# RG-LRU and soft mixture of experts on one core: one exponential for the decays of two units, and a new plan

## The chip, the cores and the metric

The kernel runs on one core of a Trainium2 chip. The metric is the device time of one execution in microseconds (us). Engines: PE (TensorE), DVE (VectorE), ACT (ScalarE), POOL (GpSimd) and SP (SyncE, which only issues transfers here). Each engine runs its own instructions strictly in the order in which they were written; semaphores hold an instruction until what it reads is there.

## The reference, cut to what matters

```python
# B, S, D = 4, 5056, 256; 8 experts, 4 slots each, hidden width 1024; all float32
log_a = 8 * sigmoid(r_gate) * log(clip(sigmoid(a_param)))      # negative
a_t   = exp(log_a)                                             # the decay
norm  = sqrt(max(1 - a_t * a_t, 1e-6))
xg    = norm * sigmoid(i_gate) * x
for t in range(S):                                             # a scan along the sequence
    h = a_t[:, t] * h + xg[:, t];  y[:, t] = h
x = y.reshape(B * S, D)                                        # 20224 tokens
logits = x @ phi                                               # 32 slots
d = softmax(logits, over tokens);  slot_input = d.T @ x
slot_out[e] = relu(slot_input[e] @ w1[e]) @ w2[e]              # per expert
out = softmax(logits, over slots) @ slot_out
```

## The kernel before, in words

**Tiling.** The 20224 tokens are 40 *quads* of 512 tokens (the last has 256). A *unit* is two quads, but the first and the last unit have one; there are 21 units, and a *chunk* is two units (`CHUNKS`), the last one. The three inputs come in quads of 512 KB, tokens on partitions. PE transposes them so that the 256 channels lie on partitions in two halves `h` and time runs along the row.

**One unit, step by step** (task names of the plan and lines of the profile):

- `TR` (L559, PE): transposes r into a double PSUM buffer `pair`; `SR` (L570, ACT): tanh of it into the decay tile `A`, a buffer of the class `b`. A sigmoid is had from tanh here.
- `EX` (L612, ACT): the exponential with a scale and a bias per channel, in place, one instruction per half, so two per unit over 1024 elements each.
- `SQ` (L623, POOL): squares the decay into `N`. `RT` (L639, ACT): the root, over both halves at once (2048 elements).
- `SI` (ACT): the gate i, in one of three ways by the letter of `IV` for the unit. S is a sigmoid (L583); P is tanh (L585) and a correction `P1` on POOL (L592); E is tanh, whose correction is put into the sum: PE transposes and adds two tiles. `U` (L601, POOL): gate times x.
- `TU` (L658, PE): transposes that product into `pair`. `ST` (L675, DVE): times the root. `SC` (L692, DVE): the scan, one per half.
- `TY` (L716, PE) turns y back to tokens on partitions, two blocks of 128 tokens at a time, and `YC` copies it out of PSUM, on DVE (L732) or ACT (L730), whichever the plan gives it.
- For each group of four quads: `LG` (L772, PE) the logits, `LE` (L785, DVE) a running maximum, `LD`, `TE`, `ES` (L826, ACT) their exponentials, `AC` (L846, PE) the weighted sum, `AE` (L862, DVE) its accumulation.

**After the scans** the partial sums of four column groups are merged (`MT` to `SL`, L1023 to L1050), PE runs the experts' two layers (L1087, L1135), and the token-side softmax is multiplied with the slots' outputs (`CT` to `OT`, L1204 to L1292), copied out of PSUM (`OE`, L1304 on ACT, L1306 on DVE) and stored (`OD`, L1316).

**Tables.** ACT needs another function table for exp and tanh, for sigmoid, for sqrt; tanh is in the first two. A change of table is an instruction of its own, shown under the line that needs it.

**What sets the order.** `Planner` is a list scheduler that runs when the program is built. Each task has an engine, a duration and a latency that the author wrote down, its dependencies, a priority and the buffers it takes. The planner walks through time with those durations and hands out buffers; the order in which tasks begin in that plan is the order in which they are written into each engine's queue. ACT's main tasks don't follow priorities: their sequence `act_seq` is built from `phases`, for each chunk tanh and exponentials, then the sigmoids, then the roots. Loads follow the same sequence on SP's queue, with i and x of a quad side by side. Tasks of ACT outside the sequence (copies, `ES`) are put between by rules in `pick_act`.

**Buffers.** `st` (7 of 512 KB) hold r and i, `b` (16 of 1 MB) hold x, `A` and `N`, `yn` (8) hold y; in PSUM there are 3 `pair` and 2 single banks. A unit's decays and roots lie in whichever `b` buffer is free.

## Time and profile before

| | |
|---|---|
| time, median of 3 runs | 311.07 us (311.02 to 311.43) |
| the profiled execution | 311.99 us, of which 310.2 are its span |
| busy PE, DVE, ACT, POOL | 263.0, 253.2, 251.8, 216.6 us |
| moved by DMA | 78.94 MB read, 20.71 MB written |
| mean granted TensorE clock | 0.968 |

The span is what lies between the first and the last instruction. A row of a timeline gives the start in us from the span's start, the length, the engine, the line, the operation, what it writes and reads, how often, and in brackets how long the engine had stood idle before it and what ended that. A row of a group gives, behind the bar, busy us in all and the mean ns of one, then the idle time before the group. A row of waits gives us in all, how many, and the longest. A row of stages gives start and end, length, then busy us of each engine with its count of instructions, the granted TensorE clock, the DMA engines' share and GB/s.

### The profile page before, as it was taken

The page shows a single profiled execution, that of the slowest core. Times are in us where ns is not written, and L with a number is a line of the kernel's source. Part 1 is how long each engine was busy: PE and PEld are TensorE (multiplying, and loading weights), DVE is VectorE, ACT ScalarE, POOL GpSimd, SP SyncE. Part 2 cuts the span into 40 slices and gives each one's busy share as a digit, 9 for nine tenths or more (in the row PEclk, how much of TensorE's full clock was granted, in tenths as well). Part 3 has the DMA queues.
Part 4 walks back from the last instruction along what each step waited for, and adds up shares of the span by engine and source line. Part 5 has one row for each costly group of instructions (what it writes and reads, how often), then busy time and mean ns, then how long its engine had stood idle before and what let it go on. Part 6 is the DMA issues. An engine that isn't in the chain of part 4 may idle for free.

```text
span 310.2 us, 5828 instructions
## 1 busy us (share of the span) xinstructions
PE 263.0 (85%) x2181; PEld 199.5 (64%) x2181; DVE 253.2 (82%) x319; ACT 251.8 (81%) x282; POOL 216.6 (70%) x162
## 2 busy tenths in 40 slices
PE   4979959689698995977969979879998999999890
PEld 3979857675564854856647547564555578878770
DVE  0236579899999999888999999999987359999870
ACT  6699999999999999899899999999330038899560
POOL 4598979968979999999597999994304503347200
PEclk9999999799999999897999999979999999999995
DMA  6999649899997786768979978879999309999997
GB/s 228 416 408 403 244 164 409 335 363 359 391 411 282 295 296 238 277 250 298 410 268 300 368 257 309 272 262 398 404 386 386 130 0 379 401 406 406 394 408 284
DMA packets 30288, 100.03 MB, mean 322 GB/s; under 512 B 3378, under 2 KB 3380, under 8 KB 30260
## 3 DMA queue, kind: packets, MB, share of 16 engines
q1 hardware_dynamic: 30256, 99.66, 85.0%
q8 instruction: 17, 0.28, 0.3%
q14 instruction: 11, 0.09, 0.1%
q10 hardware_dynamic: 4, 0.00, 0.0%
HBM read 78.94 MB, written 20.71 MB: 321 GB/s over the span
## 4 chain that ended last, share of the span: by engine, by line
PE 35%; DVE 27%; ACT 18%; DMA 9%; issue 6%; POOL 2%; SPq 0%; DVEq 0%; ACTq 0%; POOLq 0%
DVE b L692 9%; DVE pair L675 7%; PE pair L658 6%; PE pair L559 5%; DMA out_dram<-st 5%; PE bank L1292 5%; DMA st<-in_r_gate_dram 4%; ACT b L639 3%; ACT b L612 3%; ACT b L570 3%; DVE yn L732 3%; PE one L716 3%; PE one L772 2%; PE one L1135 2%; ACT st L583 2%
## 5 line engine op out<-in xcount | busy, mean ns | idle before, releaser
L601 POOL TENSOR_TENSOR b<-st,b 128x1024 f32<-128x1024 f32 (+1 forms) x36 | 84.3, 2359 | 0.5
L692 DVE TENSOR_TENSOR_SCAN b<-b,b,pair 128x1024 f32<-128x1024 f32 (+4 forms) x40 | 82.4, 2063 | 0.5
L623 POOL TENSOR_TENSOR b<-b 128x1024 f32<-128x1024 f32 (+1 forms) x40 | 72.7, 1835 | 13.6 <-ACT b L612 12.0
L675 DVE SCALAR_TENSOR_TENSOR pair<-b,pair 128x1024 f32<-128x1024 f32 (+2 forms) x42 | 48.4, 1156 | 16.8 <-PE pair L658 7.8
L559 PE MATMUL pair<-ident,st 128*128 128x128 f32 x316 | 45.6, 290 | 14.4 <-DVE b L692 6.4
L559 PEld LDWEIGHTS pair<-ident,st 128*128 128x128 f32 x316 | 37.1, 148 | 22.6 <-DVE b L692 10.3
L612 ACT ACTIVATE b<-b,ca 128x1024 f32<-128x1024 f32 (+2 forms) x42 | 48.8, 1190 | 0.4
L658 PE MATMUL pair<-ident,b 128*128 128x128 f32 x316 | 45.5, 287 | 1.9 <-DVE b L692 1.7
L570 ACT ACTIVATE b<-pair 128x1024 f32<-128x1024 f32 (+1 forms) x40 | 40.1, 1010 | 5.8 <-PE pair L559 5.7
L716 PE MATMUL one<-ident,b 128*128 128x128 f32 x232 | 37.0, 295 | 8.1 <-DVE yn L732 4.7
L658 PEld LDWEIGHTS pair<-ident,b 128*128 128x128 f32 x316 | 37.8, 148 | 8.8 <-issue 5.1
L732 DVE COPY yn<-one 128x512 f32<-128x512 f32 x53 | 34.9, 684 | 4.0 <-PE one L716 3.9
L716 PEld LDWEIGHTS one<-ident,b 128*128 128x128 f32 x232 | 27.9, 149 | 15.5 <-DVE yn L732 7.8
L1292 PE MATMUL bank<-bd,hT 128*128 128x512 f32 x120 | 33.2, 401 | 1.0 <-DVE hT L1282 0.9
L639 ACT ACTIVATE b<-b 128x2048 f32<-128x2048 f32 (+2 forms) x19 | 33.3, 1794 | 0.3 <-POOL b L623 0.2
L1235 POOL TENSOR_TENSOR b<-b,rs_all 128x512 f32<-128x512 f32 (+2 forms) x11 | 10.6, 961 | 26.1 <-DVE rs_all L1227 21.6
L1292 PEld LDWEIGHTS bank<-bd,hT 128*128 128x128 f32 x120 | 21.7, 188 | 5.6 <-DVE hT L1282 1.2
L772 PE MATMUL one<-b,phi_sb 128*32 128x512 f32 (+1 forms) x164 | 24.3, 587 | 0.3 <-DVE yn L732 0.3
L846 PE MATMUL one<-yn,eS 128*32 128x257 f32 x304 | 22.8, 384 | 0.2 <-ACT eS L826 0.2
L1304 ACT COPY st<-bank 128x512 f32<-128x512 f32 x33 | 18.7, 594 | 4.3 <-PE bank L1292 3.7
L592 POOL TENSOR_SCALAR st<-st,half_sb 128x1024 f32<-128x1024 f32 (+1 forms) x14 | 15.2, 1092 | 9.9 <-ACT st L585 9.9
L1280 ACT CAST hT<-bank 128x512 fp32r<-128x512 f32 (+1 forms) x10 | 5.8, 579 | 19.7 <-PE bank L1269 19.6
(138 smaller groups left out, 436.0 us busy)
## 6 DMA issues: line engine op xcount, KB each, us to landing
st<-in_i_gate_dram SPq DMA_DIRECT2D x39, 512.0 KB, 5.3
b<-in_x_dram SPq DMA_DIRECT2D x39, 512.0 KB, 6.3
st<-in_r_gate_dram SPq DMA_DIRECT2D x38, 512.0 KB, 6.2
out_dram<-st SPq DMA_DIRECT2D x37, 512.0 KB, 5.3
b<-in_moe_w_dram SPq DMA_DIRECT2D x26, 512.0 KB, 9.3
st<-in_moe_w_dram SPq DMA_DIRECT2D x6, 512.0 KB, 4.5
st<-in_r_gate_dram SPq DMA_DIRECT2D x3, 256.0 KB, 2.9
out_dram<-st SPq DMA_DIRECT2D x3, 256.0 KB, 4.6
```

What stands on the lines that cost most here:

```text
L559: nc.tensor.transpose(out=o[:, m, :], in_=raw("r", q)[:, m * D + h * P : m * D + (h + 1) * P], identity=ident,)
L570: nc.scalar.activation(dst, t(rp)[:, :, :c], AF.Tanh, scale=0.5)
L601: eng.tensor_tensor(out=o, in0=a, in1=b, op=ALU.mult)
L612: nc.scalar.activation(v, v, AF.Exp, scale=ca[:, h : h + 1], bias=ca[:, h : h + 1])
L623: eng.tensor_tensor(out=t(Nb[p])[:, h, :c], in0=v, in1=v, op=ALU.mult)
L639: nc.scalar.activation(v, v, AF.Sqrt, bias=quarter if f != 1.0 else f, scale=-f)
L658: nc.tensor.matmul(o[:, m, :], raw(nm, q)[:, m * D + h * P : m * D + (h + 1) * P], ident, is_transpose=True, start=(nm == nms[0] and m == ...
L675: nc.vector.scalar_tensor_tensor(v, t(Nb[p])[:, h, :c], 0.5e-3 if gate_of(quads(p)[0]) == "E" else 1e-3, v, op0=ALU.max, op1=ALU.mult)
L692: nc.vector.tensor_tensor_scan(dst, dst, flat()[:, s0:s1], init, op0=ALU.mult, op1=ALU.add)
L716: nc.tensor.transpose(out=flat()[:, b * D + h * P : b * D + (h + 1) * P], in_=t(A[p])[:, h, o : o + P], identity=ident,)
L732: nc.vector.tensor_copy(out=dst, in_=v)
L1292: nc.tensor.matmul(t(op), t(hT)[:, b * P // 2 : (b + 2) * P // 2], T["bd"][part].rearrange("p i d -> p (i d)"), start=(part == 0), stop=(p ...
```

## The change

Five things are changed together.

1. **Decays side by side.** The 16 `b` buffers become 8 tiles of two. In each chunk with two full units the second unit's decay buffer is the *mate* of the first's: both are taken at once, in the two halves of one tile (`twin`, `take`). `EX` then is one instruction per half for both units, over 2x1024 elements, after the tanh of all four quads. Other buffers are handed out so that whole tiles stay free.
2. **The gates** (`IV`) are chosen anew: 13 units by sigmoid, 3 and not 2 by E, the others by P. 11 units were S before.
3. **The order in a chunk.** `PRE = 2`, `PRE0 = 3`: tanh of r for the first two quads of the next chunk (three after the first chunk) stand among the gates of this one, ahead of its roots. `SIM = 0`: the tanh gates are no longer mixed among the exponentials but follow them. `XLATE`: the loads of x of the first chunk come behind its gates' loads.
4. **Durations and priorities of the plan** change (`PEX`, the costs of `EX`, `LN` and the first loads; `TRP`, `YLAG`, `LGP`, `ACP`, `TUP`; `FILL`, which lets ACT take copies while it would wait), one `yn` buffer goes, more `b` buffers are kept back from x and `A`, and two tables shift single tasks in priority or in ACT's sequence.
5. **The first output** is stored in two halves (`ODS = 1`).

```diff
-PRE = 0
-PRE0 = 0
-IV = 'PPEESSSSSPPPSSSSPPSSP'
-YLAG = 6
+PRE = 2
+PRE0 = 3
+IV = 'PESESSSSSPPESPSSSSSSP'
+YLAG = 14
-FILL = False
-TRP = 20
+FILL = True
+TRP = 10
-TUP = 14
-ACP = 0
-LGP = 10
+TUP = 15
+ACP = -4
+LGP = 0
-N_YN = 8
-FING = 3
+N_YN = 7
+FING = 5
-XRES = 2
-ARES = 0
-SIM = 1
+XRES = 3
+ARES = 1
+SIM = 0
-PHI = 4
-XLATE = False
+PHI = 8
+XLATE = True
-EARLY = {}
-SHIFT = {}
+EARLY = {'TY37.2': 3.6, 'HP2.0': 10.0, 'SC13.0': 1.1, ...}
+SHIFT = {'SI5': 2.1, 'SR3': 1.1, 'SI27': 1.0, 'EX0.1': 4.1, ...}
+PEX = 1.03
+ODS = 1
...
+    def twin(self):
+        free = self.slots["b"]
+        return next((i for i in free if i % 2 == 0 and i + 1 in free), None)
...
+        elif b.mate is not None:
+            i = self.twin()
+            b.slot, b.mate.kept = [i], i + 1
...
-        make("b", N_B, [P, 2, 2 * QT], sb)
+        make("b", -(-N_B // 2), [P, 4, 2 * QT], sb)
+        T["b2"] = T["b"]
+        T["b"] = [b[:, i : i + 2, :] for b in T["b2"] for i in (0, 2)]
...
+    def mk_exh(p, h):
+        c = plen(p)
+        us = [p, p + 1] if p + 1 in second else [p]
+
+        def e_ex(h=h):
+            v = T["b2"][A[p].slot[0] // 2][:, h::2, :] if len(us) == 2 else t(A[p])[:, h, :c]
+            nc.scalar.activation(
+                v, v, AF.Exp, scale=ca[:, h : h + 1], bias=ca[:, h : h + 1]
+            )
+
+        EX[(p, h)] = add("ACT", f"EX{p}.{h}", 0.29 + 0.853 * c / 1024 * len(us),
+                         deps=[SR[q] for u in us for q in quads(u)] + [t_ca], ...)
...
+            cut = nb // 2 if (i * J + j) < ODS else nb
+            for k, b0 in enumerate(range(0, nb, cut)):
...
```

Three places in the built order. First ACT's queue at the start, from the second quad to the first change of table for a root. `pair` buffers hold transposed r, `st` the gate i, `b` the decays. Before:

```order
L570 ACTIVATE b_71<-pair_102 128x2x512
L585 ACTIVATE st_63<-st_63 128x1024
L612 ACTIVATE b_69<-b_69,ca 128x512
L570 ACTIVATE b_71<-pair_103 128x2x512
L585 ACTIVATE st_65<-st_65 128x1024
L612 ACTIVATE b_71<-b_71,ca 128x1024 x2
L585 ACTIVATE st_66<-st_66 128x1024
L639 ACT_TABLE_LOAD
```

And after:

```order
L621 ACTIVATE b_68<-pair_94 128x2x512
L621 ACTIVATE b_68<-pair_93 128x2x512
L685 ACTIVATE b_68<-b_68,ca 128x1024 x2
L636 ACTIVATE st_64<-st_64 128x1024
L685 ACTIVATE b_68<-b_68,ca 128x512
L636 ACTIVATE st_66<-st_66 128x1024
L621 ACTIVATE b_71<-pair_93 128x2x512
L621 ACTIVATE b_71<-pair_94 128x2x512
L636 ACTIVATE st_61<-st_61 128x1024
L621 ACTIVATE b_71<-pair_92 128x2x512
L702 ACT_TABLE_LOAD
```

The gates moved behind the exponentials of unit 1, and three tanh of the next chunk (`b_71`) moved ahead of the roots. On SP's queue the loads there are r0, r1, i0, x0, r2, i1, x1 before, and r0, r1, r2, i0, r3, i1, r4, i2, r5, x0, x1, x2 now.

Second, ACT's queue over the chunk of units 6 and 7, from the change to the table of exp and tanh to the change for the roots. Before:

```order
L570 ACT_TABLE_LOAD
L570 ACTIVATE b_74<-pair_102 128x2x512
L570 ACTIVATE b_74<-pair_103 128x2x512
L612 ACTIVATE b_74<-b_74,ca 128x1024
L570 ACTIVATE b_76<-pair_102 128x2x512
L612 ACTIVATE b_74<-b_74,ca 128x1024
L570 ACTIVATE b_76<-pair_101 128x2x512
L826 ACTIVATE eS_94<-one_96 128x512
L612 ACTIVATE b_76<-b_76,ca 128x1024 x2
L583 ACT_TABLE_LOAD
L583 ACTIVATE st_64<-st_64 128x1024
L583 ACTIVATE st_67<-st_67 128x1024
```

(two more gates follow, and then the roots). After:

```order
L621 ACT_TABLE_LOAD
L621 ACTIVATE b_74<-pair_94 128x2x512
L621 ACTIVATE b_74<-pair_92 128x2x512
L889 ACTIVATE eS_85<-one_88 128x512
L685 ACTIVATE b_74<-b_74,ca 128x2x1024 x2
L634 ACT_TABLE_LOAD
L634 ACTIVATE st_64<-st_64 128x1024
L634 ACTIVATE st_65<-st_65 128x1024
L621 ACTIVATE b_68<-pair_92 128x2x512
L634 ACTIVATE st_67<-st_67 128x1024
L634 ACTIVATE st_61<-st_61 128x1024
L621 ACTIVATE b_68<-pair_92 128x2x512
```

Two of four tanh left the front of the chunk, four exponentials became two, and two tanh of the next chunk (`b_68`) stand among the gates.

Third, PE's queue at the end of the scans: the transposes of the last quad's y (from its decay tile, `b_74` before and `b_69` now) against the weighted sums `AC` (32x257) of the last two groups. Before:

```order
L772 MATMUL one_97<-b_74,phi_sb 32x256
L846 MATMUL one_96<-yn_88,eS_95 32x257
L846 MATMUL one_96<-yn_89,eS_95 32x257
L846 MATMUL one_96<-yn_88,eS_95 32x257
L846 MATMUL one_96<-yn_89,eS_95 32x257
L1023 MATMUL bank_2177<-ident,M 1x128
L816 MATMUL bank_2178<-ident,lD_92 128x96 x2
L846 MATMUL one_96<-yn_88,eS_95 32x257
L846 MATMUL one_96<-yn_89,eS_95 32x257
L716 MATMUL bank_2179<-ident,b_74 128x128 x4
L1028 MATMUL bank_2177<-ones,mrep 128x1
L846 MATMUL bank_2180<-yn_90,eS_94 32x257 x2
```

After:

```order
L835 MATMUL one_87<-b_69,phi_sb 32x256
L779 MATMUL one_88<-ident,b_69 128x128 x4
L909 MATMUL bank_2138<-yn_77,eS_86 32x257
L909 MATMUL bank_2138<-yn_78,eS_86 32x257
L1094 MATMUL bank_2139<-ident,M 1x128
L879 MATMUL bank_2140<-ident,lD_83 128x96 x2
```

The transposes (`x4`) moved from behind the last but one group's sums to ahead of them.

More of the change, by code (lines that the diff above doesn't have):

```diff
@@ L535 @@
         xb[p].late = lambda pl, tag: len(pl.slots["b"]) > XRES
+        ib[p].late = lambda pl, tag: len(pl.slots["b"]) > XRES
+    second = set()
+    if EX2:
+        for ch in chunks:
+            full = [p for p in ch if plen(p) == 2 * QT]
+            second |= set(full[1::2])
+    for p in second:
+        A[p - 1].mate = A[p]
     yn = {q: Buf("yn", f"yn{q}") for q in range(NQ)}
@@ L585, in e_si @@
                 nc.scalar.activation(v, v, AF.Tanh, scale=0.5)
-        g = SI[q] = add("ACT", f"SI{q}", 0.07 + 0.22 * n, deps=[ld[("i", q)]], prio=q, emit=e_si,
-                        uses=[st[("i", q)]], kind="sig" if how == "S" else "tanh")
+        if two_i(p) and i:
+            g = SI[q] = SI[q - 1]
+        else:
+            qs = quads(p) if two_i(p) else [q]
+            g = SI[q] = add("ACT", f"SI{q}", 0.07 + 0.22 * n * len(qs), deps=[ld[("i", a)] for a in qs], prio=q, emit=e_si,
+                            uses=[st[("i", q)]], kind="sig" if how == "S" else "tanh")
         def e_p1():
@@ L907, with late_i, exs @@
     ahead = []
+    def late_i(q):
+        return two_i(unit[q][0]) and unit[q][1]
+    def exs(p):
+        return [] if p + 1 in second else [("EX", p - (p in second), h) for h in range(H)]
     def roots(k):
@@ L915 @@
             now = [("SR", q) for q in quads(p) if q not in ahead]
-            prev = [("EX", chunks[k][i - 1], h) for h in range(H)] if i else []
+            prev = exs(chunks[k][i - 1]) if i else []
             x += merge(prev, now)
-        x += [("EX", chunks[k][-1], h) for h in range(H)]
+        x += exs(chunks[k][-1])
         if SIM:
-            x = merge(x, [("SI", q) for q in cq[k] if gate_of(q) != "S"])
+            x = merge(x, [("SI", q) for q in cq[k] if gate_of(q) != "S" and not late_i(q)])
         phases.append(x)
@@ L941 @@
             elif it[0] == "SI":
-                order += [("i", it[1]), ("x", it[1])]
+                for q in quads(unit[it[1]][0]) if two_i(unit[it[1]][0]) else [it[1]]:
+                    order += [("i", q), ("x", q)]
         if XLATE and len(order) and k == (0 if GATES0 else 2):
```

80 lines of the change are left out of this document (53 added, 27 removed).

## Prediction

> **What bounds the kernel now.** I read the shares of the engines first, then one table of stages, then the waits, then single rows.
>
> ```profile
> PE 263.0 (85%) x2181; PEld 199.5 (64%) x2181; DVE 253.2 (82%) x319; ACT 251.8 (81%) x282; POOL 216.6 (70%) x162
> ```
>
> No engine is full over the span, so the stages are read apart. The columns are length, busy time of each engine with its count, granted TensorE clock, DMA share and GB/s.
>
> ```profile
> core 0: us, PE busy (x) PEld busy (x) DVE busy (x) ACT busy (x) POOL busy (x), PEclk, DMA share, GB/s
> 9.23:39.23 30.00, 27.11 (x239) 26.39 (x238) 13.66 (x12) 28.67 (x27) 26.90 (x15) 1.00 0.94 363
> 39.23:207.49 168.26, 139.31 (x1174) 103.71 (x1175) 159.68 (x163) 164.71 (x151) 152.80 (x83) 0.96 0.84 309
> 207.49:227.70 20.21, 19.84 (x176) 11.96 (x174) 20.06 (x23) 13.79 (x24) 8.58 (x9) 0.98 1.03 400
> 227.70:235.13 7.43, 6.32 (x51) 3.29 (x50) 4.52 (x14) 0.97 (x4) 1.05 (x2) 1.00 1.05 386
> 235.13:255.58 20.45, 20.29 (x294) 13.06 (x295) 11.79 (x26) 2.48 (x6) 7.21 (x6) 1.00 0.41 149
> 255.58:310.20 54.62, 45.29 (x237) 36.99 (x235) 42.47 (x81) 36.35 (x68) 16.43 (x16) 0.94 0.96 380
> ```
>
> The reader is to see four bounds in turn. From 39.23 to 207.49 us ACT is busy 164.71 of 168.26 and DVE 159.68: two engines share the bound, and each has little to give, 3.55 us idle on ACT and 8.58 on DVE. From 207.49 to 227.70 DVE alone is full (20.06 of 20.21): the multiply and the scans of units 18, 19 and 20. To 255.58 a chain of short PE and DVE steps runs. From there on the output transfers fill the DMA engines. So time comes out of the long stage only if both ACT and DVE are let go.
>
> ```profile
> DVE pair L675 <- PE pair L658: 7.8, 5, 2.0
> ACT b L570 <- PE pair L559: 5.7, 6, 1.6
> ```
>
> DVE's largest waits are for the transposed input of the multiply (7.8 us in five waits), ACT's for the transposed r gate (5.7 us in six). Those are what a new order can remove.
>
> **The change part by part.** *The exponentials.* 36 instructions over 1024 elements become 18 over 2x1024.
>
> ```profile
> L612 ACT ACTIVATE b<-b,ca 128x1024 f32<-128x1024 f32 x38 | 46.1, 1242 | 0.3
> L639 ACT ACTIVATE b<-b 128x2048 f32<-128x2048 f32 x17 | 31.7, 1906 | 0.3 <-POOL b L623 0.2
> L639 ACT ACTIVATE b<-b 128x1024 f32<-128x1024 f32 x1 | 1.1, 1062 | 0.0
> ...
> 32.56 2.38 ACT L612 ACTIVATE b<-b,ca 128x1024 f32<-128x1024 f32 x2
> ```
>
> Two in a row take 2.38 us where one takes 1.242, so a further one costs 1.14. No double one is in the trace; the nearest rows are the roots, which grow by 1.906 - 1.062 = 0.844 us for 1024 more elements. A double exponential in a row is then 1.14 + 0.84 = 1.98 against 2.28 for two: 0.30 saved. Bounds: 2.28, nothing saved; and 1.242 - 0.844 = 0.40 where nothing overlaps an instruction's fixed part. I take 0.30, as they stand in a row: 18 x 0.30 = 5.4 us off ACT.
>
> *Table loads.* Up to the root of unit 18 ACT has 29 loads in place of 27, because two more chunks take gates by sigmoid.
>
> ```profile
> 69.68 2.36 ACT L612 ACTIVATE b<-b,ca 128x1024 f32<-128x1024 f32 x2
> 72.06 1.28 ACT L583 ACT_TABLE_LOAD   x1
> 73.35 3.90 ACT L583 ACTIVATE st<-st 128x1024 f32<-128x1024 f32 x4
> ...
> 203.61 3.71 ACT L639 ACTIVATE b<-b 128x2048 f32<-128x2048 f32 x2
> ```
>
> The load at 72.06 is 1.28 us and the gate after it starts 0.01 us later, so 2 x 1.29 = 2.6 us come back. The Trainium skill, "ScalarE: Activation LUTs", section "What ACT_TABLE_LOAD costs", adds a drain of about 1.38 us to the 1.28 at every switch to another set; by that page the two would cost about 5.3 us, an estimate. Here the exponentials ended at 69.68 + 2.36 = 72.04, the load began 0.02 us later and the gate 0.01 us after it: the trace has no such gap, and the sum keeps 2.6.
>
> *The rest of ACT up to that root:* the last unit's tanh moved ahead of it (0.5) and one more copy (0.5). Net on ACT: -5.4 + 2.6 + 0.5 + 0.5 = -1.8 us. The root of unit 18 ends at 203.61 + 1.86 = 205.5 now.
>
> *The order within a chunk.* Two of the next chunk's four tanh now run before the roots, so exponentials follow the load after two tanh, not four. That lets POOL's squares begin earlier, and half of the transposes of r have a whole phase to be ready in: it is against ACT's 5.7 us. Take the window 9.23 to 207.49: ACT idles 1.33 + 3.55 = 4.9 us there. All, half or none may go; half is 2.4. Root 18 then ends at 205.5 - 1.8 - 2.4 = 201.3.
>
> *The start.* r0, r1, r2 are loaded first, each x of the first chunk after nine gate loads, and three tanh of the next chunk stand ahead of the first roots.
>
> ```profile
> 7.22 1.97 PE L559 MATMUL pair<-ident,st 128*128 128x128 f32 x8 [1.12 <-DMA st<-in_r_gate_dram]
> 13.14 1.02 ACT L570 ACTIVATE b<-pair 128x1024 f32<-128x1024 f32 x1 [1.24 <-PE pair L559]
> 37.19 3.90 ACT L639 ACTIVATE b<-b,quarter 128x2048 f32<-128x2048 f32 x2
> ...
> 20.73 1.29 DVE L675 SCALAR_TENSOR_TENSOR pair<-b,pair 128x512 f32<-128x512 f32 x2 [7.69 <-ACT b L639]
> 38.40 0.69 DVE L732 COPY yn<-one 128x512 f32<-128x512 f32 x1 [3.14 <-PE one L716]
> 39.23 1.23 DVE L675 SCALAR_TENSOR_TENSOR pair<-b,pair 128x1024 f32<-128x1024 f32 x1
> ...
> 35.13 3.77 POOL L623 TENSOR_TENSOR b<-b 128x1024 f32<-128x1024 f32 x2
> 56.63 7.04 POOL L601 TENSOR_TENSOR b<-st,b 128x1024 f32<-128x1024 f32 x3
> ```
>
> The wait of 1.24 at 13.14 is for r2, which came sixth and now comes third; it goes. At 363 GB/s 0.52 MB take 1.44 us, so x0, eight transfers behind r1 (there at 7.22), lands near 7.2 + 8 x 1.44 = 18.7 and is multiplied and transposed before the first root is out; were it later, each us would push DVE's first multiply by one. Until the first root ACT does three tanh more, 2.8 us (1.02 each, less some overlap), so DVE's first multiply moves from 20.73 to about 22.3. Up to the end of root 2 (39.1 now) ACT has two tanh and a load more and two exponentials merged twice: +1.9 + 1.3 - 0.5 - 1.24, so 40.5. Unit 2 now takes sigmoid, and its products stand on POOL behind four squares: the first square at about 28.3, four of them at 1.88 each (3.77 for two) to 35.8, the gates done then, two products at 2.35 (7.04 for three) to 40.6, a transpose of about 1 us: unit 2's multiply starts at about 42, not 39.23. That costs DVE 2.8 us, partly filled by the copies for which it waited 3.14 us at 38.40.
>
> *DVE from unit 2 to unit 18.* Counted in the order, 56 copies out of PSUM stand there and not 63; all else is equal in number.
>
> ```profile
> 24.98 1.29 DVE L732 COPY yn<-one 128x512 f32<-128x512 f32 x2 [0.73 <-PE one L716]
> ```
>
> A copy in a row costs 1.29 - 0.69 = 0.60, so DVE has 159.68 - 4.2 = 155.5 us of work. From 42 this gives unit 18's multiply at 197.5 with no idle, 206.1 with all 8.58, 201.8 with half. ACT says 201.3 and from there a wait for the transpose of up to the 2.0 that it is now (205.5 to 207.49); half of it gives 202.3, which I take: **5.2 us** off, between 1.4 (206.1) and 8.5 (ACT without idle, 205.5 - 1.8 - 4.9 = 198.8, and 0.2 to the multiply). Both rest on POOL, which has six gate corrections of 1.1 us fewer and one product of 2.35, 9.0 us in all; DVE makes that product in the 7.69 us before its first multiply. If squares or products are late on POOL, the multiply is what is late next (first rival). PE gets 16 transposes more for a third unit that sums the tanh gate there, 16 x 0.11 = 1.8 us of the 29 that it idles in the long stage.
>
> *The last scans.* One copy fewer stands between the multiply of 18 and the last scan: **0.6 us**.
>
> *The merge.* The last transposes of y are issued ahead of the last two groups' sums and not behind the first of them.
>
> ```profile
> 230.45 0.33 ACT L826 ACTIVATE eS<-bank 128x192 f32<-128x192 f32 x1 [0.79 <-PE bank L816]
> 231.54 0.69 DVE L732 COPY yn<-bank 128x512 f32<-128x512 f32 x1
> 231.74 1.60 PE L846 MATMUL bank<-yn,eS 128*32 128x257 f32 x12
> ```
>
> The last sum waits for the copy that ends at 232.2 though its weights were there at 230.8; about 1.2 us, of which I take **1.0**, between 0 and 1.2. Expert weights stand behind it:
>
> ```profile
> 242.00:244.00 2.00, 2.00 (x44) 1.23 (x40) 0.48 (x1) 0.00 (x0) 2.00 (x3) 1.00 0.48 176
> ...
> 246.20 4.52 PE L1135 MATMUL one<-b,b 128*32 128x256 f32 x80
> ```
>
> The transfers end near 243, and the last of five experts in these 4.52 us starts near 249.8, so 6.8 us of gain ahead of it are covered even if the weights come no earlier; past that they would set the end.
>
> *The outputs.* The first output leaves in two halves.
>
> ```profile
> 254.48 0.59 ACT L1304 COPY st<-one 128x512 f32<-128x512 f32 x1 [0.92 <-PE one L1292]
> 254.96 0.59 ACT L1304 COPY st<-bank 128x512 f32<-128x512 f32 x1
> ```
>
> It is issued at 255.58, where the last stage of the table begins, since it waits now for both copies (255.55); the first half is ready at 255.07, so the stream starts **0.5 us** earlier, between 0 and 0.6; the one extra issue is covered by transfers in flight. The moved copies there change which engine does them; with 380 GB/s over the stage I cost them at nothing.
>
> Sum: 5.2 + 0.6 + 1.0 + 0.5 = 7.3. The profiled execution took 311.99 (span 310.2), so it would take 304.7; the median of the runs, 311.07, is 0.92 below, so **303.8**.
>
> **The rivals.** *POOL late in every chunk (slower).* Both first squares now wait for the first double exponential and all products stand behind four squares. DVE waits five times now for transposed products, 2.0 us at most. With 2.0 at each of nine chunks that is 18 us of idle on DVE: 42 + 155.5 + 18 = 215.5, 8.0 later, less the other 2.1: 317.0. It decides from 12 us, 1.35 a chunk. For it: eight chunks take sigmoid, not six. Against: POOL idles 15.5 us in the long stage and has those 9.0 us less to do.
>
> *The stalls stay.* If the waits merely move, ACT's -1.8 is all that the long stage gives: 311.07 - 1.8 - 2.1 = 307.2. For it: three double PSUM buffers as before, and one buffer for y fewer.
>
> *The double exponential costs two.* Then 5.4 us come back: 309.2. Against it: the root over 2048 elements costs 1.906 and not 2 x 1.062.
>
> *Every switch of tables hides a pause.* If ACT had to empty itself at a switch for as long as the load takes, two more would cost 2.6 more: 306.4. The rows at 72.06 speak against it. This is how the page above counts.
>
> **How the numbers follow.** Forecast 0.60; stalls stay 0.20; POOL late 0.12 (of it 0.02 within 0.2% of now, about what a measurement of this kernel can tell from no change); double costs two 0.05; table pause 0.03. Faster 0.60 + 0.20 + 0.05 + 0.03 = 0.88, same 0.02, slower 0.10. The best end is 8.5 + 0.6 + 1.2 + 0.6 = 10.9 off, 300.2; the worst of the faster cases 1.4 + 0.6 = 2.0, 309.1. I give 300.2 to 309.2, which leaves out POOL late and a few in a hundred below.
>
> **What would show it.** The double exponential near 2.0 to 2.1 us; unit 2's multiply near 42; unit 18's near 202.3 with DVE idle about 4 in between; ACT waiting under 3 us for transposes of r; the first output near 248.5 and the output stage still near 54 us. It would be wrong if DVE's waits on the transposed products grow past 12 us in all, or if the output stage grows, where I costed the new order at nothing.

## The result and the profile after

The changed kernel took 306.89 us (median of 6 runs, 304.62 to 308.83); the kernel before, timed with it, 311.25 (median of 6). The ratio is 0.987, interval 0.983 to 0.990: 1.3% faster, clear of no change. Put on a chip a second time it gave 307.83 against 310.64, ratio 0.990, interval 0.983 to 0.997. The forecast was 303.8, the range 300.2 to 309.2. Of the 7.3 us of gain that were forecast, the medians show 4.4, and 2.8 the second time.

The profiled execution took 304.62 us, where the sum said 304.7. Runs of both kernels scatter with the granted clock: the changed one took 304.62 to 305.76 at 0.995 and 306.64 to 310.96 at 0.979 to 0.986; its profiles show the first kind.

First, as before, the shares of the engines, and the table of stages, cut at the same events: unit 2's multiply, unit 18's multiply, the end of the last scan, the first expert product, the first output.

```profile
PE 256.7 (85%) x2181; PEld 191.9 (63%) x2181; DVE 251.1 (83%) x313; ACT 250.1 (83%) x273; POOL 207.3 (68%) x154
```

```profile
core 0: us, PE busy (x) PEld busy (x) DVE busy (x) ACT busy (x) POOL busy (x), PEclk, DMA share, GB/s
9.20:41.21 32.01, 26.17 (x226) 24.26 (x225) 17.19 (x17) 31.26 (x27) 22.90 (x12) 1.00 0.96 373
41.21:201.43 160.22, 134.17 (x1174) 97.70 (x1173) 155.39 (x155) 159.49 (x138) 146.81 (x79) 1.00 0.85 316
201.43:220.90 19.47, 18.65 (x175) 11.53 (x173) 19.36 (x23) 13.86 (x25) 9.17 (x9) 1.00 1.00 390
220.90:227.95 7.05, 5.96 (x50) 3.11 (x49) 3.88 (x13) 1.44 (x5) 1.05 (x2) 1.00 1.05 388
227.95:247.64 19.69, 19.69 (x292) 12.67 (x293) 11.05 (x24) 2.38 (x6) 7.30 (x6) 1.00 0.53 195
247.64:302.80 55.16, 46.23 (x239) 37.38 (x237) 43.17 (x82) 35.87 (x69) 16.50 (x16) 0.97 0.95 377
```

Read the third column from the right with the first: the long stage fell from 168.26 to 160.22 us, ACT is busy for 159.49 of it (0.73 idle) and DVE idles 4.83, where it idled 8.58. The granted clock in the stage is 1.00, where it was 0.96.

| us | before | forecast | after |
|---|---|---|---|
| unit 2's multiply starts | 39.23 | about 42 | 41.21 |
| to unit 18's multiply | 168.26 | 160.3 | 160.22 |
| unit 18's multiply starts | 207.49 | 202.3 | 201.43 |
| to the end of the last scan | 20.21 | 19.6 | 19.47 |
| to the first expert product | 7.43 | 6.4 | 7.05 |
| to the first output | 20.45 | 19.95 | 19.69 |
| outputs | 54.62 | 54.62 | 55.16 |
| span | 310.2 | 302.9 | 302.8 |

So of the 7.4 us of span 6.06 came ahead of unit 18's multiply, 0.74 in the last scans, 0.38 in the merge, 0.76 up to the first output, and 0.54 went back in the output stage.

The two waits that were to shrink did (5.7 and 7.8 us before):

```profile
ACT b L621 <- PE pair L610: 2.5, 2, 1.3
DVE pair L738 <- PE pair L721: 5.3, 5, 1.7
```

Not all of this lies in the long stage. Three of ACT's six waits before stand in the first 14 us (1.56, 1.65 and 1.24 of the 5.7 us); the stage itself held 1.23, and now holds none. DVE's waits inside the stage fell from 5.97 us (four) to 2.53 (three).

The new instruction, as a group (count, busy us, mean ns) and in a row with the table load ahead of it:

```profile
L685 ACT ACTIVATE b<-b,ca 128x2048 f32<-128x2048 f32 x18 | 37.3, 2101 | 0.1
...
58.07 3.73 ACT L702 ACTIVATE b<-b 128x2048 f32<-128x2048 f32 x2
61.81 1.28 ACT L621 ACT_TABLE_LOAD   x1
63.11 1.94 ACT L621 ACTIVATE b<-pair 128x1024 f32<-128x1024 f32 x2
...
65.41 4.09 ACT L685 ACTIVATE b<-b,ca 128x2048 f32<-128x2048 f32 x2
```

One double exponential is 2.10 us; two in a row take 4.09, so a further one costs 1.98 to 1.99, as forecast (1.98). And the load begins 0.01 us after the roots end, the tanh 0.02 us after the load: no pause at a switch.

The start. DVE's first multiply, POOL's four squares and the products behind them, and unit 2's multiply:

```profile
21.88 1.29 DVE L738 SCALAR_TENSOR_TENSOR pair<-b,pair 128x512 f32<-128x512 f32 x2 [3.02 <-ACT b L702]
28.29 7.45 POOL L672 TENSOR_TENSOR b<-b 128x1024 f32<-128x1024 f32 x4 [4.68 <-ACT b L685]
35.70 4.69 POOL L656 TENSOR_TENSOR b<-st,b 128x1024 f32<-128x1024 f32 x2
41.21 1.23 DVE L738 SCALAR_TENSOR_TENSOR pair<-b,pair 128x1024 f32<-128x1024 f32 x1 [1.70 <-PE pair L721]
```

The squares begin at 28.29 (forecast 28.3) and end at 35.74, the products at 40.39: the chain that was forecast.

The end of the long stage. POOL's last products, unit 18's root, and DVE ahead of unit 18's multiply:

```profile
195.18 9.35 POOL L656 TENSOR_TENSOR b<-st,b 128x1024 f32<-128x1024 f32 x4
196.43 1.91 ACT L702 ACTIVATE b<-b 128x2048 f32<-128x2048 f32 x1
199.63 1.29 DVE L795 COPY yn<-pair 128x512 f32<-128x512 f32 x2 [0.83 <-PE pair L779]
201.43 2.35 DVE L738 SCALAR_TENSOR_TENSOR pair<-b,pair 128x1024 f32<-128x1024 f32 x2
```

The root ends at 198.34, three us earlier than forecast (201.3), but the multiply follows 3.1 us behind it and not 1.0: the first two of the four products are done at 195.18 + 4.68 = 199.9 and have to be transposed (1.1 us), and DVE uses the time for copies and for a step of the token-side softmax (0.68 us at 200.84), behind which the multiply stands in its queue.

### The profile page after: what moved, and what is told of

It reads as the page before. It is cut to its first block, busy times and chain, and to the rows that moved or that the text cites. A ratio compares the mean times of both kernels' runs of the same rounds, so it can differ in the third digit from the quotient of the medians.

```text
span 302.8 us, 5814 instructions
## 1 busy us (share of the span) xinstructions
PE 256.7 (85%) x2181; PEld 191.9 (63%) x2181; DVE 251.1 (83%) x313; ACT 250.1 (83%) x273; POOL 207.3 (68%) x154
## 4 chain that ended last, share of the span: by engine, by line
ACT 52%; PE 25%; DVE 9%; issue 7%; DMA 4%; POOL 0%; SPq 0%; DVEq 0%; ACTq 0%
ACT b L702 10%; ACT b L621 10%; ACT b L685 9%; PE bank L1363 8%; ACT st L634 6%; ACT L702 4%; DVE b L755 4%; ACT st L636 3%; ACT L621 3%; ACT L634 3%; PE one L1363 2%; PE bank L1206 2%; DVE pair L738 2%; DMA st<-in_r_gate_dram 2%; PE bank L1340 2%
## 5 line engine op out<-in xcount | busy, mean ns | idle before, releaser
L656 POOL TENSOR_TENSOR b<-st,b 128x1024 f32<-128x1024 f32 (+1 forms) x33 | 76.3, 2339 | 0.2
L755 DVE TENSOR_TENSOR_SCAN b<-b,pair 128x1024 f32<-128x1024 f32 (+6 forms) x28 | 52.2, 1883 | 0.2
L610 PE MATMUL pair<-ident,st 128*128 128x128 f32 x316 | 42.6, 281 | 11.5 <-ACT b L621 5.4
L721 PEld LDWEIGHTS pair<-ident,b 128*128 128x128 f32 x316 | 34.5, 141 | 23.6 <-ACT b L621 7.7
L685 ACT ACTIVATE b<-b,ca 128x2048 f32<-128x2048 f32 (+3 forms) x24 | 42.5, 1796 | 0.2
L755 DVE TENSOR_TENSOR_SCAN b<-b,b,pair 128x1024 f32<-128x1024 f32 (+2 forms) x20 | 40.9, 2047 | 0.3
L779 PE MATMUL one<-ident,b 128*128 128x128 f32 x224 | 33.0, 278 | 0.6 <-DVE b L755 0.6
L795 DVE COPY yn<-one 128x512 f32<-128x512 f32 x47 | 30.8, 683 | 2.7 <-PE one L779 2.5
L634 ACT ACTIVATE st<-st 128x1024 f32<-128x1024 f32 x26 | 25.9, 1048 | 0.1
L1377 DVE COPY st<-bank 128x512 f32<-128x512 f32 x26 | 17.3, 680 | 4.3 <-DMA out_dram<-st 2.9
```

Of the source, the lines that this page charges most:

```text
L610: nc.tensor.transpose(out=o[:, m, :], in_=raw("r", q)[:, m * D + h * P : m * D + (h + 1) * P], identity=ident,)
L634: nc.scalar.activation(v, v, AF.Sigmoid)
L656: eng.tensor_tensor(out=o, in0=a, in1=b, op=ALU.mult)
L685: nc.scalar.activation(v, v, AF.Exp, scale=ca[:, h : h + 1], bias=ca[:, h : h + 1])
L721: nc.tensor.matmul(o[:, m, :], raw(nm, q)[:, m * D + h * P : m * D + (h + 1) * P], ident, is_transpose=True, start=(nm == nms[0] and m == ...
L755: nc.vector.tensor_tensor_scan(dst, dst, flat()[:, s0:s1], init, op0=ALU.mult, op1=ALU.add)
```

## The experiments

Ten kernels were run, and the two of the comparison again. For stretches of a profile the start of unit 2's multiply is the zero, since the first transfers arrive up to 3 us later in some executions (first multiply between 21.88 and 25.18). The stretch from unit 2's to unit 18's multiply repeats well: 160.22, 160.18 and 160.23 us in three profiles of the changed plan (the changed kernel twice, and with one output), at a granted clock of 1.00 in each.

### Single exponentials in the same plan

```diff
-            v = T["b2"][...][:, h::2, :] if len(us) == 2 else t(A[p])[:, h, :c]
-            nc.scalar.activation(v, v, AF.Exp, ...)
+            for u in us:
+                v = t(A[u])[:, h, :c]
+                nc.scalar.activation(v, v, AF.Exp, ...)
```

> The changed kernel with its plan kept; each double exponential is issued as two single ones (one for each unit) at the same place. Theory of the prediction: 18 x 0.30 = 5.4 us go back on ScalarE, which had only 0.7 us idle in the long stage of the changed kernel, so unit 18's multiply moves from 201.4 to about 206.5 and the profiled span from 302.8 to about 308. Rival: VectorE and GpSimd set the pace there, VectorE has 4.8 us idle and a square can start after the first of the two single exponentials, so less than 2 us comes back (span below 305). Rival: pairing also ordered everything else, and all of the gain goes (span 310).

Measured: 310.19 us (median of 12), ratio to before 0.997 (0.993 to 1.001); profiled span 309.0. The stretch, then its part up to the end of unit 18's root and what follows, and the exponentials as a group:

```profile
41.56:207.28 165.72, 134.99 (x1174) 98.71 (x1172) 155.87 (x155) 165.04 (x155) 149.44 (x80) 0.99 0.83 310
...
41.56:203.14 161.58, 131.38 (x1152) 95.10 (x1149) 153.98 (x152) 160.92 (x151) 145.30 (x78) 1.00 0.83 311
...
203.14:207.28 4.14, 3.61 (x22) 3.61 (x23) 1.89 (x3) 4.12 (x6) 4.14 (x3) 0.70 0.70 250
...
L686 ACT ACTIVATE b<-b,ca 128x1024 f32<-128x1024 f32 x38 | 44.6, 1240 | 0.0
```

The changed kernel's 18 double ones and two single ones of this size take 37.3 + 2.4 = 39.7 us, these 38 take 44.6: 4.9 us for the 18 pairs, 0.27 each. The changed kernel from unit 2's multiply to the same root:

```profile
41.21:198.34 157.13, 131.61 (x1151) 95.14 (x1149) 153.13 (x152) 156.40 (x135) 143.72 (x78) 1.00 0.85 318
```

Up to there 16 of the pairs run, at a clock of 1.00 in both kernels. ACT is 4.52 us busier (16 x 0.27 = 4.3) and the root ends 4.45 us later (161.58 to 157.13): nearly every us comes through. The whole stretch is 5.50 longer, but the last 1.05 of it goes with the clock and not with the exponentials: from the root to the multiply it is 4.14 us where it was 3.09, at a clock of 0.70 against 1.00, and the multiply waits 0.96 us for its transposes, a row of 16 on PE that takes 3.38 us where it took 1.91. The theory holds: it moved the multiply by 5.1 us (201.4 to 206.5). What the order is worth without the pairing can't be read from 165.72 against 168.26 of before, since the clock differs there too (0.99 and 0.96). Unit 18's multiply starts at 207.28, where it started at 207.49 before.

### The first output in one piece

```diff
-ODS = 1
+ODS = 0
```

> The changed kernel with the first output in one piece again; the plan ahead of it is the same. Theory of the prediction: the stream of outputs starts 0.5 us later and ends 0.5 us later (span 303.3). Rival, from the changed kernel's profile: the output stage there is 0.54 us longer than before, so the earlier start was given back behind the first output, and the end does not move (span within 0.1 us of 302.8).

Measured: 306.34 us (median of 6), ratio 0.984 (0.979 to 0.990); with 306.89 for the changed kernel no difference. From the first expert product on:

```profile
228.48:248.64 20.16, 20.16 (x294) 13.07 (x295) 11.52 (x25) 2.85 (x7) 7.29 (x6) 1.00 0.52 190
248.64:303.40 54.76, 45.97 (x236) 36.93 (x235) 42.67 (x81) 35.39 (x68) 16.49 (x16) 0.97 0.96 379
```

The first output starts 0.47 us later (20.16 against 19.69), and the stage behind it is 0.40 shorter: together 74.92 against 74.85. The rival holds by the stages. Taken alone, the profiled span of 303.4 is what the theory said, but this execution began late: its first multiply stands at 22.45, that of the changed kernel at 21.88, and the 0.6 us more of span are there. Over the first 4.4 us, cut at the same point of the plan, the DMA share is 0.77 with the early half and 0.72 without; over the next 8 us it is 1.02 in both. What follows the first output sets when the transfers become dense.

### The pairing alone, with the old order

Gates, orders and buffer counts of before; `EX2 = True` and the paired buffers. The costs of `EX`, `LN` and the first loads stay those of the changed kernel.

> The kernel before with the double exponential and the paired buffers alone; gates, orders, buffer counts and costs of the planner are those of before. Theory: ScalarE has 18 x 0.30 = 5.4 us less work but its waits for the transposed r (5.7 us) and VectorE's for the transposed products (7.8 us) belong to the old order, so only part comes through: 2 to 3 us faster than before. Rival: ScalarE alone sets the pace, all 5.4 us come through (span near 305). Rival: the exponentials now come both at the end of a chunk, GpSimd starts its squares later, and the kernel is no faster or slower (span 310 or more).

Measured: 334.92 us (median of 6), ratio 1.073 (1.066 to 1.080): slower, as the second rival said, but by far more than any of them had a reason for. ACT's wait and the stretch:

```profile
ACT b L621 <- PE pair L610: 18.9, 17, 3.3
...
51.82:223.45 171.63, 139.36 (x1086) 101.55 (x1084) 156.65 (x162) 154.20 (x130) 147.66 (x81) 0.92 0.75 279
```

ACT does have its work cut (154.20 us in the stretch) but idles 17.4 us of it, and waits 18.9 us in all for the transposed r, where before it waited 5.7. A pair needs two neighbouring buffers of class `b` at once, and the x quads use the same class. DMA share in the stretch is 0.75 (0.84 before), and unit 2's multiply starts 12.6 us late (51.82 against 39.23). Which of the buffer counts and orders causes it was not taken apart, so that the buffers are the cause is argued and not shown.

### The order alone, with single exponentials planned anew

```diff
-EX2 = True
+EX2 = False
```

> The changed kernel with single exponentials and unpaired buffers, planned anew; gates, orders and costs are the new ones. Theory: ScalarE has 5.4 us more work than in the changed kernel, which it cannot hide: 2 us faster than before (span near 308). Rival: the order was the gain, and 5 us or more stay (span 305 or less). Rival: the two table loads more of the new gates (2.6 us) are not paid for without pairing, and the kernel is as slow as before or slower (span 310 or more).

Measured: 330.75 us (median of 6), ratio 1.063 (1.058 to 1.067). The stretch is 166.44 us, near that of the first experiment (165.72). The loss lies behind it, between the first expert product and the first output (32.20 us in place of 19.69):

```profile
239.41:271.61 32.20, 25.06 (x316) 16.75 (x316) 17.77 (x38) 5.50 (x10) 7.98 (x7) 0.89 0.31 114
...
256.50 0.41 DVE L1230 TENSOR_SCALAR hs<-bank 128x256 int32<-128x256 int32 x1
267.08 1.09 PE L1340 MATMUL bank<-ident,st 128*128 128x128 f32 x4 [2.88 <-DVE b L1289]
```

The experts' result is there at 256.9, and the weights' first transpose for an output (L1340), which in the changed kernel begins just ahead of that (243.20 and 244.77), comes 10 us behind it. That is a plan that doesn't fit, no price of the exponentials. That the two tables of local orders are to blame, since they name single instructions of another plan, is likely but not shown. This run and the one before it answer nothing about the parts by themselves.

### Single exponentials with an order of their own

`EX2 = False`, twelve numbers of the planner changed (among them `XRES` 3 to 1 and `ALAG` 2 to -16), fewer sigmoid gates (11 units and not 13), and tables of local orders chosen for this kernel.

> Single exponentials and unpaired buffers again, but with numbers of the planner and a table of local orders that were chosen for this kernel, where the run before (order alone) kept those that were chosen for the paired one. Theory: pairing saves 18 x 0.30 = 5.4 us on ScalarE, which no order can give back, so it stays 3 to 5.5 us above the changed kernel (span 306 to 308.5), and the 20 us by which the order alone was slower belonged to tables that fit another plan. Rival: without pairing the new order does not work at all (span above 312). Rival: a good order makes pairing needless (span below 304.5).

Measured: 310.3 us (median of 12), ratio 1.001 (0.997 to 1.005); profiled span 308.1.

```profile
40.88:203.84 162.96, 139.30 (x1207) 104.66 (x1205) 154.32 (x154) 161.92 (x151) 146.55 (x79) 0.98 0.83 313
```

The theory holds: 3.4 us above the changed kernel by the medians, 5.3 by the profiles, and the 20 us belonged to numbers and tables chosen for another plan; which of the two was not taken apart. In the stretch ACT is full again (161.92 of 162.96). The stretch is 2.74 us above the changed kernel's. So this order gives back a part of what single exponentials cost in the first experiment, and then pays 1.75 more in the outputs (56.91 against 55.16), 1.05 in the merge and 0.2 in the last scans.

### Without the local orders

```diff
-EARLY = {'TY37.2': 3.6, 'HP2.0': 10.0, ...}
+EARLY = {}
-SHIFT = {'SI5': 2.1, 'SR3': 1.1, ...}
+SHIFT = {}
```

> The changed kernel with both tables of local orders empty (the instructions that are moved one by one), planned anew; pairing, gates and all other numbers kept. Theory, after the run with the order alone: the local orders hold the plan together, and without them the kernel loses 3 us or more, in the stretch from the last scan to the first output above all. Rival (the prediction costed the moved copies at nothing): within 1 us of the changed kernel.

Measured: 309.99 us (median of 12), ratio 1.000 (0.996 to 1.004); profiled span 308.9.

```profile
42.64:203.90 161.26, 137.11 (x1183) 101.69 (x1182) 156.19 (x157) 160.50 (x139) 146.41 (x79) 0.98 0.83 315
...
223.52:232.65 9.13, 7.94 (x64) 4.42 (x62) 5.18 (x15) 1.79 (x5) 1.05 (x2) 1.00 1.05 387
...
252.32:308.90 56.58, 46.23 (x239) 37.21 (x237) 43.62 (x83) 36.43 (x68) 16.52 (x16) 0.95 0.93 367
```

Of the 6.1 us of span 1.4 lie ahead of unit 2's multiply (1.15 of them ahead of the first, where executions differ), 1.0 in the stretch, 0.2 in the last scans, 2.1 in the merge (9.13 against 7.05) and 1.4 in the outputs. The theory holds in size; the place was half wrong, since the experts' part (19.67) is untouched. By the medians it is 3.1 us, about as much as the pairing (3.3). The kernel was planned anew, so this is the price of the tables and of all that moves with them. Of the 1.0 us in the stretch 0.83 stand in its first chunk (22.06 us against 21.23), where the clock is 0.92. Either of the two taken away leaves a kernel that is no faster than the one before.

### More work on VectorE

```diff
+                if h == 0 and 3 <= p <= 16:      # ahead of a unit's first multiply
+                    nc.vector.scalar_tensor_tensor(spare, spare, 1e-3, spare, op0=ALU.max, op1=ALU.mult)
```

> The changed kernel with its plan kept; VectorE gets 14 idle instructions over 128x256 (one ahead of the first multiply of each of units 3 to 16), about 14 x 0.41 = 5.7 us of work that nothing needs. Theory (ScalarE alone sets the pace of the long stage: VectorE idles 4.8 us there, and 9.9 us with single exponentials): at most 2.5 us slower, and VectorE's idle in the stage falls. Rival (my prediction's reading, that ScalarE and VectorE share the bound): all or nearly all of the 5.7 us comes through, span 307 to 308.5.

Measured: 318.52 us (median of 6), ratio 1.027 (1.021 to 1.033). The added instructions (min, median, max in ns), and the stretch:

```profile
L741 DVE SCALAR_TENSOR_TENSOR spare<-spare x14: 514/944/1821, 52.6 to 194.1; 128x256 f32<-128x256 f32 x14
...
43.92:213.92 170.00, 139.47 (x1175) 101.81 (x1174) 167.26 (x169) 161.72 (x139) 148.83 (x79) 0.97 0.80 299
```

They took 13.4 us in all, where 5.7 were meant, and the stretch is 9.8 us longer. My theory of this run (ScalarE alone sets the pace) falls: only 3.6 of 13.4 us were absorbed. (A part of the 9.8 may be the clock's, which was 0.91 from 80 to 120 us.) Since the size was off, it was run again with memsets, which read nothing:

```diff
+                if h == 0 and 3 <= p <= 16:
+                    nc.vector.memset(spare, 0.0)             # 128x384
```

> As the run with more work on VectorE, but the 14 idle instructions are memsets over 128x384, which read nothing: there the idle ones took 0.51 to 1.82 us each (13.4 us in all, where 5.7 were meant) while GpSimd was in a square or product. A memset over 128x256 took 0.272 us, so 14 x 0.41 = 5.7 us. Theory (ScalarE and VectorE share the bound; VectorE idles 4.8 us in the long stage, but in front of single instructions): 3 to 5.5 us of the 5.7 come through, span 306 to 308.5. Rival (ScalarE alone sets the pace, and the 12 us of the earlier run came from the blocked port): under 2 us, span below 305. If the instructions again take far more than 0.41 us, it was not the two operands that were held up.

Measured: 309.31 us (median of 12), ratio 0.997 (0.993 to 1.000).

```profile
L740 DVE MEMSET spare<- x14: 378/378/378, 52.9 to 187.3; 128x384 f32 x14
...
44.04:207.01 162.97, 137.95 (x1175) 101.00 (x1173) 159.87 (x170) 160.58 (x139) 147.13 (x79) 0.98 0.83 312
```

14 x 0.378 = 5.3 us more work make the stretch 2.75 longer, DVE's idle time falls from 4.83 to 3.10. That lies between the two theories: about half comes through. The clock was below 1.00 in parts of this stretch too; in the five chunks where it was 1.00 in both kernels (66.12 to 168.32 here, 62.44 to 163.08 in the changed kernel) ten memsets, 3.78 us, cost 1.56.

### More work on GpSimd

```diff
+                    nc.gpsimd.tensor_tensor(out=spare, in0=spare, in1=spare, op=ALU.mult)   # ahead of a chunk's first product
```

> The changed kernel with its plan kept; GpSimd gets one idle product over 128x512 (1.05 us) ahead of the first product of each chunk from the third to the tenth, 8 x 1.05 = 8.4 us, and a memset ahead of the second chunk's. Rival of the prediction (POOL late in every chunk) put the point from which it decides at 1.35 us a chunk; GpSimd idles 13.4 us in the long stage of the changed kernel. Theory: most of it is covered, less than 2.5 us slower. Rival: the products are already what VectorE waits for (5.3 us in five waits), so each us is paid in most chunks: 5 us or more slower.

Measured: 307.73 us (median of 12), ratio 0.991 (0.987 to 0.995).

```profile
42.40:202.69 160.29, 135.58 (x1175) 97.75 (x1173) 155.38 (x155) 159.48 (x139) 154.16 (x87) 1.00 0.84 315
```

Eight of them took 8.3 us, GpSimd's idle time in the stretch falls from 13.4 to 6.1, and the stretch is the same to 0.07 us. The theory holds: at 1.04 us a chunk products are not late.

### Two table loads fewer

The sigmoid of units 2, 16 and 17 becomes a tanh, and its correction is left out, so the gates of these units are not those of the reference.

```diff
-            if how == "S":
+            if how == "S" and p not in (2, 16, 17):
```

> The changed kernel with its plan kept; the sigmoid gates of units 2, 16 and 17 are taken by tanh without the correction that it needs (that part of the computation is left out), so that two chunks need no sigmoid table: 30 table loads in place of 32. Theory: 2 x 1.29 = 2.6 us less on ScalarE, of which 1 to 2.6 comes through (VectorE has 4.8 us idle in the long stage to give): 300.2 to 301.8 for the span. Rival (a switch also empties the engine for about as long as the load, 2.6 each): 5 us less on ScalarE, span below 300. Rival (VectorE is the bound now): within 0.7 us of the changed kernel.

Measured: 307.24 us (median of 6), ratio 0.988 (0.983 to 0.993); the profiled span of 305.8 has a first multiply that is 3.3 us late.

```profile
44.52:204.36 159.84, 133.90 (x1174) 97.64 (x1173) 155.32 (x155) 159.12 (x138) 147.38 (x79) 1.00 0.84 318
```

One of the two loads stands ahead of unit 2's multiply, and from the first multiply to that one it is 19.34 us, as in the changed kernel (19.33): that load cost nothing. By the rows of the changed kernel POOL's squares and products set that multiply. The other stands in the stretch, which is 0.38 shorter for 1.28 us less on ACT (ACT's busy time falls by 0.37 only, since it goes on to work that stood behind the stretch). The rival with VectorE as the bound holds, on the strength of that one load: less work on ScalarE alone now buys little.

### The two kernels again

> The changed kernel once more, beside the others on their chip: 304.6 to 308.8 us, 0.983 to 0.990 of the kernel before, as in the first comparison. If it is 0.980 or less the first six runs were on the slow side; if 0.993 or more, the profiled execution (7.4 us faster than that of before) was a lucky one.

Measured as told above: 0.990 (0.983 to 0.997), profiled span 304.0, stretch 160.23.

> The kernel before once more, for a second profile of it. In three profiles of the changed plan (the changed kernel twice, and with one output) the stretch from unit 2's multiply to unit 18's took 160.18 to 160.23 us; the one profile of before has 168.26, at a granted clock of 0.96 there. If the 8.0 us between them belong to the change, the stretch is again 167.5 to 169 whatever the clock; if a part belongs to the clock, it falls below 167 where the clock is 0.985 or more.

Measured: 315.19 us in this one run, clock 0.966.

```profile
40.15:210.60 170.45, 140.83 (x1176) 104.22 (x1176) 159.98 (x162) 163.84 (x150) 152.87 (x83) 0.95 0.82 305
```

The stretch is 2.2 us longer than in the first profile of before, so the theory that it is 167.5 to 169 whatever the clock falls; no profile of before at a clock of 0.985 or more was had, so the other is untested as it was put. But the stretch holds eight chunks, and between the two profiles the clock of single chunks differs. The last two chunks, in the first profile of before:

```profile
167.17:187.66 20.49, 17.58 (x155) 12.30 (x153) 20.31 (x23) 20.20 (x20) 18.16 (x12) 1.00 0.84 304
187.66:207.49 19.83, 16.50 (x142) 12.24 (x140) 19.02 (x19) 19.53 (x20) 19.83 (x11) 0.94 0.84 276
```

And in this one:

```profile
170.23:191.63 21.40, 18.53 (x155) 14.04 (x153) 20.68 (x22) 21.10 (x21) 19.11 (x13) 0.92 0.84 309
191.63:210.60 18.97, 15.65 (x144) 11.20 (x141) 18.93 (x18) 17.87 (x18) 18.97 (x10) 1.00 0.75 267
```

The first of these chunks is 0.91 us longer at 0.92 than at 1.00, the second 0.86 longer at 0.94. The instructions are the same; in the longer chunks DVE idles, 0.16 us for PE ahead of each of three copies from 187.92 on here, and 0.77 ahead of the multiply at 207.49 in the first profile. Three other chunks had 1.00 both times: two of them took the same time (19.82 and 20.26 us), the third differs by 0.38 (23.32 and 23.70).

## Why the prediction was right, and where not

*What bounds the kernel.* Right, and for the changed plan shown from both sides. There 4.52 us more on ScalarE cost 4.45, 5.3 more on VectorE cost 2.75, 8.3 more on GpSimd 0.07, and 1.28 less on ScalarE gave 0.38. For the kernel before it is read from the shares alone. Both engines have to be let go; the change did that, with 5.2 us off ScalarE in the stage (164.71 to 159.49) and 4.3 off VectorE (159.68 to 155.39; forecast 155.5). Of ScalarE's 5.2 us 2.6 only moved ahead of the stage (28.67 to 31.26), which leaves 2.6 where the forecast had 1.8.

*The exponentials.* Right: 0.27 each by the groups, forecast 0.30; the 16 pairs ahead of unit 18's root came through there as 4.45 us.

*The stall half.* Its number came out by luck. It held half of ACT's idle time against the waits for transposed r, but most of those 5.7 us stand in the first 14 us of the kernel, and only 1.23 in the stage. ACT's idle time in the stretch is 0.73, less than the forecast let stand, and its root 18 came 3 us earlier than forecast; the wait between root and multiply, which I took as 1.0, is 3.1. The two errors cancel in unit 18's multiply (201.43 for 202.3), which is set by transposes and DVE's queue and not by the root. DVE's idle time is 4.83 (forecast about 4).

*The start* came as forecast, 41.21 for 42, by the chain that was forecast, and *the last scans* too (0.74 for 0.6).

*The merge* was mis-sized: 1.0 forecast, 0.38 measured. The wait for the copy did go, but the weights (ready at 223.84) now find PE in the middle of the group ahead:

```profile
223.34 1.06 PE L909 MATMUL bank<-yn,eS 128*32 128x257 f32 x8
223.51 0.33 ACT L889 ACTIVATE eS<-bank 128x192 f32<-128x192 f32 x1 [0.33 <-PE bank L879]
224.65 1.50 PE L909 MATMUL bank<-yn,eS 128*32 128x257 f32 x16
226.21 0.48 DVE L925 SCALAR_TENSOR_TENSOR accS<-accS,dm,bank 96x257 f32<-96x257 f32 x1 [0.36 <-PE bank L909]
```

PE ends those eight at 224.40 and then runs 16 to 226.15, where before 12 stood at the end. PE's own queue took the place of the wait for the copy.

*The outputs.* 0.5 forecast, nothing gained. The half output does leave 0.5 us earlier, but the step failed where it took the end of the stream to move with its start: the stream starts, and then waits for the next ones. The kernel with one output shows it.

*The local orders, costed at nothing,* are the step that the prediction had no place for. The prediction named a growing output stage as a sign of being wrong; against before it grew by 0.54 only. But the kernel planned without the tables is 6.1 us longer by the span, 2.1 of it in the merge and 1.4 in the outputs, and 3.1 by the medians. So the tables hold what the new order would otherwise lose there.

*The rivals.* POOL late in every chunk: it was to decide from 1.35 us a chunk, and another 1.04 a chunk on top of the changed kernel cost 0.07 us in the stretch, so it was far off. The stalls stay: ACT's wait for r in the stage fell from 1.23 us to none, DVE's for products from 5.97 to 2.53, in part by the clock. The double exponential costs two: one takes 2.10 us, where two single ones in a row take 2.38. A pause at each switch: the rows at 61.81 have none; the run with two loads fewer can't tell, since VectorE hid what it saved.

*The clock,* for which the sum has no term, is the second piece of luck. Three of DVE's four waits for transposed products in the stage before (1.99 us at 62.62, 0.97 at 124.95, 1.07 at 146.91) stand at the end of, or just behind, some us in which the granted clock was low (0.57, 0.75, 0.64). The us ahead of the first:

```profile
54.00:58.00 4.00, 1.36 (x11) 0.89 (x10) 4.00 (x5) 3.97 (x5) 4.00 (x3) 1.00 1.00 395
58.00:62.00 4.00, 4.00 (x24) 4.00 (x22) 2.59 (x5) 3.98 (x3) 4.00 (x3) 0.57 0.72 277
```

PE has little to do (1.36 of 4 us), then gets work at a clock of 0.57, and DVE falls idle (2.59 of 4 us busy) until the transposes are done. The prediction took these waits for a matter of the order alone. Four of the eight chunks of before ran below 1.00 (0.93, 0.95, 0.89, 0.94), and all eight of the changed kernel at 1.00. If each low chunk costs the 0.9 us by which the two chunks above differ, some 3.5 of the 8.0 us in the stretch went with the clock: an estimate from those two chunks (4 x 0.9). The clock isn't chance alone: in 64 timed runs of before it was 0.962 to 0.988, in the 12 of the changed kernel 0.979 to 0.995. Whether the new order raises it, by leaving PE fewer gaps, no run shows.

*From the profile to the median.* The sum was right for the profiled execution (304.7 for 304.62), and the step to the median failed: I took 0.92 off, because the profiled execution of before was that much above its median. That of the changed kernel is 2.3 below its own. The gain is 7.4 us between two profiled executions and 4.4 between the medians (2.8 in the second comparison). The two profiles have clocks of 0.968 and 0.995; 1174 matmuls of the long stage took 139.31 us in one and 134.17 in the other. Six runs of each kernel have clocks between 0.983 and 0.986: their medians are 310.0 and 307.5, a gain of 2.5 us. The clock's exact share stays open.

## What to carry to other kernels

Where two engines share a stage, a profile says how much each idles, but only more or less work on one of them, in an unchanged plan, tells what a us is worth: here 1.0 for one more on ScalarE, 0.3 for one less, 0.5 for one more on VectorE. A plan that was tuned by single instructions can't be split into its parts by planning anew with one part off: two such runs were 19 and 23 us slower than before and said nothing about the parts, while emitting another instruction in the same plan gave the price to 0.1 us. Before a wait for PE is put down to the order, read the granted clock in the us ahead of it. And take a gain between profiled executions for what it is, if their granted clocks differ.

## What the hardware showed that was not expected

A VectorE instruction over 128x256 with both operands in SBUF took 0.51 to 1.82 us, 0.96 in the mean, while GpSimd was at work; the longest is this one, and GpSimd's squares over it:

```profile
74.79 1.82 DVE L741 SCALAR_TENSOR_TENSOR spare<-spare 128x256 f32<-128x256 f32 x1
...
72.58 5.78 POOL L674 TENSOR_TENSOR b<-b 128x1024 f32<-128x1024 f32 x3
...
76.28 2.08 POOL L674 TENSOR_TENSOR b<-b 128x1024 f32<-128x1024 f32 x1
```

The multiply over the same width with one operand in PSUM takes 0.41, and the memsets took 0.378 each time, so as far as these three forms show it is the two SBUF operands that wait, for about one square (1.90 us) at most: the instruction of 74.79 ends at 76.61, 0.33 us after the square that ran at its start gave way to the next (76.28). The Trainium skill, "SBUF — State Buffer", section "SBUF: two separate sides", says that VectorE with two SBUF inputs and a GpSimd instruction that reads SBUF lock the shared port pair against each other for a whole instruction; these rows agree. GpSimd is held up a little in turn: the square that follows, at 76.28, takes 2.08 us, and the mean of the squares in this run is 1.93 (1.90 in the changed kernel).
